# Fetching attention heads one by one with a casting DMA, and running TensorE on ones before the first inputs come

## The chip, the cores and the metric

One core of a Trainium2 chip. The metric is the device time of one execution in microseconds (us). Each kernel was executed several times, with one execution under the hardware profiler; timed kernels were run in rounds beside the kernel before on the same chip. A ratio is the mean time of one kernel's fast runs over the mean of the other's fast runs of the same rounds, so it is not quite the ratio of the medians that are quoted.

## The reference

Attention over 4 batches, 8 heads, 768 positions, 64 columns a head; some heads ("retrieval") see all earlier positions, the others ("streaming") only the first 4 positions and a window of 64. Then a two-layer block on the result:

```python
def reference(q, k, v, is_retrieval, n_sink, window, w_in, w_out):
    scores = q @ k.T / 8                       # per batch and head
    mask = causal where is_retrieval else causal & (sink | window)
    a = softmax(where(mask, scores, -1e9))
    x = (a @ v) as (3072, 512)
    h = x @ w_in                               # 512 -> 2048
    return (h - tanh(h)) @ w_out               # 2048 -> 512, float32
```

q, k, v and the weights come as float32 in device memory.

## The kernel before

The kernel works on 12 tiles of 256 positions (three a batch). A small planner inside it takes every instruction with a guessed duration, simulates the engines, and so fixes each engine's order; at run time each engine goes through its own list in that order. Batch 0 (tiles 0 to 2) takes the heads as they come. From tile 3 on the heads are sorted so that retrieval heads come first ("ranked"), so that half of the head pairs need only the window; the sort is worked out on the chip from the flags, and the rank-to-head table sits in registers.

Before, a ranked tile is fetched by plain DMAs, six a tile, and GpSimd (POOL) then casts float32 to float16 head by head, picking the head by a register:

```python
for i in blocks:                               # 2 blocks of 128 positions, q, k, v each
    op("SP", ..., lambda: nc.sync.dma_start(
        out=raw_of(nm, t)[:, i, h0 : h0 + nh, :],
        in_=src[b, h0 : h0 + nh, s0 : s0 + 128, :].rearrange("h p d -> p h d")))
...
at = bass.ds(regs["POOL"][rank], 1)            # cast_ranked: 8 casts of q and k, 8 of v
nc.gpsimd.tensor_copy(out=t16[t % 2][:, :, :, rank : rank + 1, :],
                      in_=raws["rqk", t][0]()[:, :, :, at, :])
```

Weights and tiles 1 and 2 come by casting DMAs that GpSimd issues. The three forms of them that this document compares:

```python
nc.gpsimd.dma_start(out=t16[...][:, i, x, :, :],              # q, k, v: 128 x 8 runs of 256 B
    in_=src[b, :, s0 : s0 + 128, :].rearrange("h p d -> p h d"))
nc.gpsimd.dma_start(out=w()[:],                               # w_in: 128 x 4 runs of 2 KB
    in_=moe_w_in[:, c0 : c0 + n].rearrange("(cb p) f -> p cb f", p=128))
nc.gpsimd.dma_start(out=w()[:].rearrange("p i m -> p (i m)"), # w_out: 128 runs of 8 KB
    in_=moe_w_out[j * 512 : (j + 1) * 512, :].rearrange("(p i) m -> p (i m)", p=128))
```

After the casts, two DMA transposes a tile (queue SP) put q and k in place, GpSimd "spreads" parts of v into `vf`, and TensorE scores, sums values and runs the two layers.

The softmax here doesn't subtract the row's maximum and nothing guards it: scores larger than these inputs give would overflow.

Of the kernel before, what the change touches and what calls it, by code (L numbers as in the profile page):

```python
# [12 lines left out]
TT = 256  # L13
# [3 lines left out]
class Plan:  # L17
# [16 lines left out]
    def op(self, eng, ns, fn, r=(), w=(), dma=None, prio=None, port=False, after=None, behind=None):  # L34
        i = len(self.ops)
        deps = set() if after is None else {after}
        for k in r:
            if k in self.writer:
                deps.add(self.writer[k])
            if k[0] in self.PSUM:  # L40
                deps.update(j for j in self.readers.get(k, ()) if self.ops[j][0] != eng)
            self.readers.setdefault(k, []).append(i)
# [16 lines left out]
    def run(self):  # L59
# [45 lines left out]
        while len(order) < n:  # L105
# [34 lines left out]
            for u in followers[i]:  # L140
                ready[u] = max(ready[u], t + ns)
                left[u] -= 1
                if not left[u]:
                    enqueue(u)
            if dma:
                packets, each = dma
                rings["POOL" if e == "POOL" else "SP"].append(
                    [i, t + ns + (1200 if e == "POOL" else 300), each, packets * each / 16]
                )
            else:  # L150
                finish(i, t + ns + self.RESULT[e])
# [6 lines left out]
def kernel(  # L158
# [35 lines left out]
    RAW, PT, XB, GB, XTB, THB, OB = 2, 3, 3, 3, 3, 3, 3  # L194
# [28 lines left out]
    gate = const.tile([1, 1], FP16, name="gate")  # L223
# [33 lines left out]
    def program(first):  # L257
# [30 lines left out]
        def paired(nm, t):  # L288

            return nm != "v" and t == 0  # L290

        def load(t, names="qkv", halves=(None,), blocks=range(NB), after=None):

            b, g = divmod(t, NG)
            for half in halves:
                h0, nh = (0, H) if half is None else (half * HH, HH)
                for nm in names:
                    src = {"q": q, "k": k, "v": v}[nm]
                    tag = "rv" if nm == "v" else "rqk"
                    if (tag, t) not in raws:  # L300
                        idx = rot[tag] = rot.get(tag, -1) + 1
                        shape = [128, NB, H, D] if nm == "v" else [128, NB, 2, H, D]
                        raws[tag, t] = (
                            lazy(raw_pool, shape, FP32, tag, f"raw_{tag}{t}"), idx
                        )
                    if paired(nm, t):
                        op(
                            "SP", max(420, 128 * nh * 1.1),
                            lambda nm=nm, src=src, h0=h0, nh=nh: nc.sync.dma_start(
                                out=raw_pairs(nm, t)[:, h0 : h0 + nh, :, :].rearrange(  # L310
                                    "p h e d -> p h (e d)"
                                ),
                                in_=src[b, h0 : h0 + nh, g * TT : (g + 1) * TT, :].rearrange(
                                    "h (p e) d -> p h (e d)", e=NB
                                ),
                            ),
                            w=[
                                key for x in (range(2) if half is None else (half,))
                                for key in raw_keys(nm, t, x)
                            ],  # L320
                            dma=(128 * nh, 26.0), after=after,
                        )
                        continue
                    for i in blocks:
                        s0 = g * TT + i * 128
                        op(
                            "SP", max(420, 128 * nh * 1.1),
                            lambda nm=nm, i=i, src=src, s0=s0, h0=h0, nh=nh: nc.sync.dma_start(
                                out=raw_of(nm, t)[:, i, h0 : h0 + nh, :],
                                in_=src[b, h0 : h0 + nh, s0 : s0 + 128, :].rearrange("h p d -> p h d"),  # L330
                            ),
                            w=[
                                key for x in (range(2) if half is None else (half,))
                                for key in raw_keys(nm, t, x, (i,))
                            ],
                            dma=(128 * nh, 18.3), after=after,
                        )
# [13 lines left out]
        def raw_keys(nm, t, half, blocks=range(NB)):  # L351
            tag = "rv" if nm == "v" else "rqk"
            return [(tag, raws[tag, t][1], nm, half, i) for i in blocks]
# [11 lines left out]
        def load_cast(t, w_after=(), names="qkv"):  # L365

            b, g = divmod(t, NG)
            for nm in names:
# [13 lines left out]
                if nm == "v":  # L382
                    for i in range(NB):
# [3 lines left out]
                            dma=(128 * H, 18.5),  # L387
                        )
                    continue
                for i in range(NB):  # L390
                    behind(
                        930, lambda fn=fn, i=i: fn((i,)), r=w_after,
                        w=[key for half in range(2) for key in t16_keys(nm, t, half, (i,))],
                        dma=(128 * H, 18.5),
# [37 lines left out]
        for half in range(2):  # L432
            load(0, "qk", (half,))
            load(0, "v", (half,))
        if first:

            op("POOL", 204, lambda: nc.gpsimd.memset(ones[:], 1.0), w=["ones"])
            op(
# [98 lines left out]
        def by_rank(after):  # L537

            def dve(ns, fn, r, w):
                op("DVE", ns, fn, r=r, w=w, after=after)  # L540
# [82 lines left out]
                r=["A4", "A40", "A41", "A43"], w=["mS"], port=True, after=after,  # L623
# [4 lines left out]
                r=["mS3"], w=["mS"], port=True, after=after,  # L628
            )
            for e, et in (("POOL", Engine.Pool), ("DVE", Engine.DVE)):  # L630
# [7 lines left out]
                op(e, 900, get, r=["perm"], w=["regs" + e])  # L638
# [9 lines left out]
        def t16_keys(nm, t, half, blocks=range(NB)):  # L648
            return [("t16", t % 2, nm, half, i) for i in blocks]

        def cast_qk(t, engines, halves=range(2)):

            for half in halves:
                for nm, es in zip("qk", engines):
                    hs = slice(half * HH, half * HH + HH)
                    cast_op(
                        es[half], NB * HH * D,
                        lambda nm=nm, hs=hs: t16[t % 2][:, :, "qk".index(nm), hs, :],
                        lambda nm=nm, hs=hs: raw_of(nm, t)[:, :, hs, :],
                        r=raw_keys(nm, t, half), w=t16_keys(nm, t, half),  # L660
                    )

        def cast_ranked(t):
# [4 lines left out]
            for half in range(2):  # L668
                for nm in ("qk", "v"):
                    for rank in range(half * HH, half * HH + HH):  # L670

                        def fn(nm=nm, rank=rank):
                            at = bass.ds(regs["POOL"][rank], 1)
                            if nm == "v":
                                nc.gpsimd.tensor_copy(  # L675
                                    out=v1s[b]()[:, lo : lo + NB, rank : rank + 1, 0:D],
                                    in_=raw_of("v", t)[:, :, at, :],
                                )
                            else:
                                nc.gpsimd.tensor_copy(  # L680
                                    out=t16[t % 2][:, :, :, rank : rank + 1, :],
                                    in_=raws["rqk", t][0]()[:, :, :, at, :],
                                )

                        op(
                            "POOL", 300 if nm == "v" else 430, fn,
                            r=["regsPOOL"] + [
                                key for x in range(2) for n_ in nm for key in raw_keys(n_, t, x)
                            ],
                            w=[("v1", b, g, half)] if nm == "v" else [  # L690
                                key for n_ in nm for key in t16_keys(n_, t, half)
                            ],
                            port=True,
                        )
            for i in range(NB):

                def turn(i=i):
# [7 lines left out]
                    r=[key for half in range(2) for n_ in "qk" for key in t16_keys(n_, t, half)],  # L705
# [83 lines left out]
        def cast_v(t, engines=("POOL", "POOL"), halves=range(2)):  # L789
# [5 lines left out]
            for half in halves:  # L795
# [4 lines left out]
                    r=raw_keys("v", t, half), w=[("v1", b, g, half)],  # L800
# [27 lines left out]
        def st_T(n, eq="DVE", ek="DVE"):  # L828
            t, hp = divmod(n, HP)
            b, g = divmod(t, NG)  # L830
            for x, (nm, e) in enumerate((("q", eq), ("k", ek))):
# [9 lines left out]
                def turn(x=x, tp=tp):  # L841
# [7 lines left out]
                    "PE", 112, turn, r=t16_keys(nm, t, hp * 2 // HP) + ["ident"], w=[key],  # L849
# [412 lines left out]
        cast_qk(0, (("ACT", "ACT"), ("ACT", "DVE")), (0,))  # L1262
        load_cast(1, [("rv", 0, "v", 0, 1)], "qk")
# [10 lines left out]
        cast_v(0, ("POOL", "POOL"), (0,))  # L1274
        cast_qk(0, (("ACT", "ACT"), ("ACT", "DVE")), (1,))
# [8 lines left out]
        cast_v(0, ("POOL", "POOL"), (1,))  # L1284
# [16 lines left out]
        else:  # L1301
            load(2)
            scale_v(0, "POOL")
        scale_v(1)
        if first:

            def wait_tile_2():
                nc.sync.dma_start(out=gate[:], in_=t16[0][0:1, 0, 1, 0, 0:1])

# [133 lines left out]
```

## Time and profile before

| | kernel before |
|---|---|
| time, median of 3 | 238.7 us |
| span of the profiled execution | 236.7 us |
| TensorE busy | 221.5 us |
| first real matmul / first hidden-layer matmul | 6.0 / 18.9 us |
| GpSimd busy | 90.5 us |

The prediction shows the page, the table of stretches and TensorE's waits. In a line of groups the columns are: line, engine, operation, output and input, count, then busy us, mean ns of one, then the idle time of the engine just before them and what ended it. The casts that the change removes, and the casting DMAs' time on GpSimd:

```profile
L680 POOL CAST t<-raw_rqk 128x256 f16 x72 | 28.5, 440 | 63.3 <-DMA raw_rqk<-in_k_dram 48.1 <-PE sc L941 15.2
L675 POOL CAST v<-raw_rv 128x128 f16 x72 | 21.1, 335 | 4.2 <-DMA raw_rv<-in_v_dram 4.2
...
L378 POOL DMA_DIRECT2D t<-in_q_dram x4 | 3.8, 963 | 0.0
...
L401 POOL DMA_DIRECT2D win<-in_moe_w_in_dram x4 | 3.0, 762 | 0.0
L415 POOL DMA_DIRECT2D wout<-in_moe_w_out_dram x4 | 2.3, 573 | 1.8 <-DMA wout<-in_moe_w_out_dram 1.6 <-DMA t<-in_q_dram 0.3
```

A run is one contiguous piece of device memory: a DMA of 1024 runs (here q) holds GpSimd for 0.96 us.

### The profile page before, as it was taken

How to read it: one execution, taken by the hardware profiler on the slowest of the kernel's cores; microseconds unless marked ns; L12 is line 12 of the kernel's file. 1: busy time of each engine (PE TensorE's matmuls, PEld its weight loads, DVE VectorE, ACT ScalarE, POOL GpSimd, SP SyncE). 2: the span in 40 equal slices, each digit the busy share in tenths (PEclk: the TensorE clock that was granted, in tenths of full speed). 3: DMA queues.
4: the chain of work that ended last, by engine and by line, in shares of the span. 5: the costliest groups of instructions: out<-in, count | busy, mean ns of one | idle time of the engine just before them, and what ended most of it. 6: DMA issues, size and time to landing. Idle time of an engine off the chain costs nothing. (4 is left out here: it accounts for less than half of the span.)

```text
span 236.7 us, 5895 instructions
## 1 busy us (share of the span) xinstructions
PE 221.5 (94%) x2220; PEld 157.8 (67%) x2220; DVE 139.0 (59%) x343; ACT 143.6 (61%) x221; POOL 90.5 (38%) x218
## 2 busy tenths in 40 slices
PE   0889899999999999999999999999999999999991
PEld 0346687756776777777676777776776777777661
DVE  1856665864488657767666655667766546443300
ACT  3668677884588387466686649537759464444320
POOL 5999420089818068480814904606300000000000
PEclk9999999999999999999999999999999999999999
DMA  5999999999997999979989695998712101310121
GB/s 128 209 140 172 204 181 204 197 228 224 206 225 182 151 248 184 227 153 206 239 168 214 136 186 130 186 171 179 134 47 66 38 31 47 90 38 9 44 89 51
DMA packets 108130, 35.29 MB, mean 149 GB/s; under 512 B 100290, under 2 KB 104642, under 8 KB 108098
## 3 DMA queue, kind: packets, MB, share of 16 engines
q1 hardware_dynamic: 92642, 28.98, 60.5%
q0 software_dynamic: 15168, 5.77, 20.7%
q8 instruction: 18, 0.29, 0.5%
q10 hardware_dynamic: 288, 0.14, 0.2%
q14 instruction: 14, 0.11, 0.2%
HBM read 27.27 MB, written 6.29 MB: 142 GB/s over the span
## 5 line engine op out<-in xcount | busy, mean ns | idle before, releaser
L1135 PE MATMUL ph<-xT,win 128*128 128x256 f16 x768 | 101.7, 273 | 0.6 <-DMA win<-in_moe_w_in_dram 0.3
L1194 PE MATMUL po<-wout,gt 128*128 128x512 f16 (+1 forms) x400 | 98.0, 371 | 0.3 <-ACT ot L1170 0.3
L1148 ACT ACTIVATE th<-ph 128x512 f32<-128x512 f32 x96 | 57.6, 601 | 59.6 <-PE ph L1135 58.2
L1155 DVE SCALAR_TENSOR_TENSOR gt<-th,ph 128x512 f16<-128x512 f32 x96 | 65.4, 684 | 44.9 <-ACT th L1148 44.4
L1135 PEld LDWEIGHTS <-win 128*128 128x128 f16 x768 | 80.0, 114 | 13.0 <-issue 1.9
L961 ACT ACTIVATE pt<-sc 128x1024 f16<-128x1024 f32 (+1 forms) x78 | 68.5, 926 | 11.4 <-PE sc L941 10.9
L1194 PEld LDWEIGHTS <-gt 128*128 128x128 f16 x400 | 36.4, 98 | 24.6 <-issue 0.9
L680 POOL CAST t<-raw_rqk 128x256 f16 x72 | 28.5, 440 | 63.3 <-DMA raw_rqk<-in_k_dram 48.1
L1030 PEld LDWEIGHTS <-pt 128*128 128x128 f16 x552 | 25.9, 98 | 10.4 <-issue 0.9
L1030 PE MATMUL av<-v,pt 128*128 128x65 f16 x304 | 26.0, 195 | 0.1
L941 PE MATMUL sc<-qk 64*128 64x128 f16 (+1 forms) x412 | 23.8, 240 | 1.7 <-DVE qk L826 1.7
L941 PEld LDWEIGHTS <-qk 64*128 64x128 f16 x412 | 13.7, 94 | 13.5 <-issue 8.9
L675 POOL CAST v<-raw_rv 128x128 f16 x72 | 21.1, 335 | 4.2 <-DMA raw_rv<-in_v_dram 4.2
L1060 DVE TENSOR_TENSOR x16t<-av,rinv 128x128 f32 x72 | 20.8, 289 | 2.3 <-DVE rinv L1050 0.3
L1030 PE MATMUL av<-vf,pt 128*128 128x65 f16 x248 | 19.6, 193 | 0.0
L1170 ACT ACTIVATE ot<-po 128x512 f32<-128x512 f32 (+1 forms) x24 | 14.3, 596 | 8.5 <-PE po L1194 8.4
L996 DVE TENSOR_TENSOR pt<-pt,m 128x1024 f16<-128x1024 f16 x16 | 12.3, 768 | 8.0 <-ACT pt L961 8.0
L1050 DVE RECIPROCAL rinv<-av 128x4 f32<-128x4 f32 x48 | 8.6, 179 | 13.4 <-PE av L1030 13.4
L986 DVE TENSOR_TENSOR pt<-pt,mS 128x512 f16<-128x512 f16 x24 | 9.8, 449 | 6.7 <-ACT pt L961 6.7
L843 PEld LDWEIGHTS <-t 128*128 128x128 f16 x48 | 3.9, 107 | 8.9 <-ACT t L644 6.8
L523 DVE TENSOR_SCALAR m<-A,thr 128x512 f16<-128x512 f16 x16 | 7.4, 501 | 1.7 <-PE sc L928 1.2
L751 POOL TENSOR_TENSOR vf<-v,rflagr 128x260 f16<-128x260 f16 x12 | 7.5, 634 | 0.0
(95 smaller groups left out, 90.8 us busy)
## 6 DMA issues: line engine op xcount, KB each, us to landing
out_dram<-ot SPq DMA_DIRECT2D x23, 256.0 KB, 2.3
raw_rqk<-in_q_dram SPq DMA_DIRECT2D x20, 256.0 KB, 4.7
raw_rqk<-in_k_dram SPq DMA_DIRECT2D x20, 256.0 KB, 4.5
raw_rv<-in_v_dram SPq DMA_DIRECT2D x18, 256.0 KB, 4.4
win<-in_moe_w_in_dram POOLq DMA_DIRECT2D x4, 512.0 KB, 8.8
wout<-in_moe_w_out_dram POOLq DMA_DIRECT2D x4, 512.0 KB, 12.4
raw_rv<-in_v_dram SPq DMA_DIRECT2D x4, 128.0 KB, 4.7
t<-in_q_dram POOLq DMA_DIRECT2D x4, 128.0 KB, 9.5
```

Of the source, the lines that this page charges most:

```text
L675: nc.gpsimd.tensor_copy(out=v1s[b]()[:, lo : lo + NB, rank : rank + 1, 0:D], in_=raw_of("v", t)[:, :, at, :],)
L680: nc.gpsimd.tensor_copy(out=t16[t % 2][:, :, :, rank : rank + 1, :], in_=raws["rqk", t][0]()[:, :, :, at, :],)
L941: nc.tensor.matmul(out=sc()[:, hh, o : o + nb * 128].rearrange("p (i c) -> p i c", c=128), lhsT=ks.rearrange("p i c -> p (i c)")[p_, jb * ...
L961: lambda pt=pt, gi=gi, wid=wid, sc=sc: nc.scalar.activation(out=pt()[:, :, 512 * gi : 512 * gi + wid], in_=sc()[:, :, 0:wid], func=AF.Exp, ...
L996: nc.vector.tensor_mul(out=pv, in0=pv, in1=m4[:, h0 : h0 + 2, 256:512].unsqueeze(2).to_broadcast([128, 2, 2, 256]),)
L1030: nc.tensor.matmul(out=av()[:, i, hh, :], lhsT=pt()[:, hh, co : co + 128], rhs=vv, start=(jb == first_jb), stop=(jb == qb),)
L1060: nc.vector.tensor_mul(out=x16s[t]()[:, :, at, :], in0=av()[:, :, hh : hh + 1, 0:D], in1=rinv()[:, :, hh : hh + 1].unsqueeze(3).to_broadca ...
L1135: nc.tensor.matmul(out=ph()[:, j, :], lhsT=w()[:, cb, c0 + fb % 4 : c0 + 512 : 4], rhs=xTs[t]()[:, cb, :], start=(cb == 0), stop=(cb == HP ...
L1148: lambda: nc.scalar.activation(out=th()[:], in_=ph()[:], func=AF.Tanh, scale=1.0 / XS),
L1155: lambda: nc.vector.scalar_tensor_tensor(out=gts[t]()[:, u * FU : (u + 1) * FU, :], in0=th()[:], scalar=-XS, in1=ph()[:], op0=ALU.mult, op ...
L1170: nc.scalar.activation(out=ot()[:, c0:c1], in_=po()[:, c0:c1], func=AF.Copy, scale=1.0 / XS)
L1194: nc.tensor.matmul(out=po()[:, c0:c1], lhsT=gts[t]()[:, f, ts * 128 : ts * 128 + 128], rhs=w_out_t[f // 4]()[:, f % 4, c0:c1], start=(f == ...
```

## The change

Its intent: take the casts of batches 1 to 3 off GpSimd by letting the DMA cast in flight, head by head, into the place of the rank; start the first tile two heads at a time; let TensorE multiply a tile of ones until q and k come, so that its clock is up by then. Six small parts go with it. Its core (cuts marked):

```diff
@@ planner: nothing slips in between two chained DMA issues
-                ready[u] = max(ready[u], t + ns)
+                ready[u] = max(ready[u], free[e])
@@ buffers
-    RAW, PT, XB, GB, XTB, THB, OB = 2, 3, 3, 3, 3, 3, 3
+    RAW, PT, XB, GB, XTB, THB, OB = 1, 4, 3, 3, 3, 3, 3
@@ first tile by pairs of heads
-        for half in range(2):
-            load(0, "qk", (half,))
-            load(0, "v", (half,))
+        for names, pairs in [("qk", (0,)), ("qk", (1,)), ("v", (0, 1)), ("qk", (2, 3)), ("v", (2, 3))]:
+            load(0, names, pairs)
@@ run-up
+            wm, key = bank([128, 512], FP32, "o", "warm")
+            def run_up():
+                for _ in range(10):
+                    nc.tensor.matmul(out=wm()[...], lhsT=ones[:], rhs=ones[:]...to_broadcast([128, 4, 128]),
+                                     start=True, stop=True)
+            op("PE", 4000, run_up, r=["ones"], w=[key])
@@ ranked tiles: cast_ranked goes, load_ranked comes
+                for rank in range(H):
+                    def fn(nm=nm, src=src, rank=rank):
+                        at = bass.ds(regs["POOL"][rank], 1)
+                        ...
+                        nc.gpsimd.dma_start(
+                            out=o,          # v1 or t16, in the place of the rank
+                            in_=src[b, at, g * TT : (g + 1) * TT, :].rearrange(
+                                "h (i p) d -> p i (h d)", p=128))
+                    behind(380, fn, r=["regsPOOL"], ..., dma=(NB * 128, 14.0), after=PACE.get((t, nm)))
@@ pacing: q, k of tile t+2 behind the scores of tile t's third head pair, v behind its fourth
+                        names = ["", "", "qk", "v"][hp]
+                            PACE[t + 2, nm] = first_S[t * HP + hp] if t > 1 else None
+                        if ranked(t + 2):
+                            load_ranked(t + 2, names)
@@ the sort of heads one tile earlier
-                if first and fast and (t, hp) == (2, 0):
+                if first and fast and (t, hp) == (1, 0):
... (keys by head pair instead of half, casts of tile 0 dealt to ACT and DVE by pair, a gate on
     tile 1's load until the second pair of k is in, guessed DMA costs)
```

## The prediction

> **What bounds the kernel now.** I read the summary page first, for who is full and when.
>
> ```profile
> PE 221.5 (94%) x2220; PEld 157.8 (67%) x2220; DVE 139.0 (59%) x343; ACT 143.6 (61%) x221; POOL 90.5 (38%) x218
> PE   0889899999999999999999999999999999999991
> ```
>
> The kernel runs on TensorE's time: empty slice 0, ragged slices 1 to 3, full from then to the last slice. A busy TensorE is not one at its peak, so I went next to the table of stretches, with bounds chosen at the first transpose (6), the first hidden-layer matmul (19) and the end of the loads.
>
> ```profile
> 0.00:6.00 6.00, 0.00 (x0) 0.00 (x0) 1.03 (x7) 2.10 (x3) 3.09 (x16) 1.00 0.53 130
> 6.00:19.00 13.00, 11.12 (x97) 5.66 (x98) 9.44 (x27) 8.94 (x16) 12.77 (x17) 1.00 1.58 167
> 19.00:30.00 11.00, 9.78 (x124) 7.26 (x125) 7.09 (x19) 8.34 (x14) 7.53 (x9) 1.00 1.28 197
> 30.00:40.00 10.00, 9.70 (x101) 8.13 (x99) 5.86 (x12) 7.09 (x14) 1.23 (x3) 1.00 1.67 192
> 40.00:70.00 30.00, 29.33 (x330) 20.78 (x329) 19.07 (x60) 21.21 (x33) 15.98 (x43) 1.00 1.12 216
> 70.00:160.00 90.00, 89.73 (x939) 64.84 (x936) 59.73 (x142) 57.31 (x86) 44.08 (x117) 1.00 0.97 185
> 160.00:232.00 72.00, 71.81 (x646) 51.12 (x638) 36.40 (x81) 38.57 (x60) 5.86 (x17) 1.00 0.25 68
> ```
>
> Columns: stretch and length, then busy us and instructions of PE, PEld, DVE, ACT, POOL, then clock, DMA share, GB/s. To see how much of "busy" is work, I took the matmuls of each stretch from the groups by form and charged each its array time[...]. Sums: 5.9 us of work in the 13 of 6 to 19; 9.0 in the 11 of 19 to 30; 9.7 in 10; 29.0 in 30; then 91 in 90 and 72.5 in 72, that is, full. So what can be won is 6 us of empty start, 7 us in the head, 2 in 19 to 30, about 1.3 up to 70, and the 5 us after the last matmul, which the change doesn't touch. Nothing can be won from 70 to 232.
>
> Then the waits of TensorE over the span:
>
> ```profile
> PE tp0q L843 <- ACT t L644: 6.0, 1, 6.0
> PE sc L941 <- DVE qk L826: 1.7, 3, 0.7
> PE xp L1108 <- DVE x L1074: 1.1, 3, 0.6
> PE tp0k L843 <- ACT t L644: 0.5, 1, 0.5
> PE ph L1135 <- DMA win<-in_moe_w_in_dram: 0.3, 1, 0.3
> ```
>
> The casts and loads of batches 1 to 3 stand nowhere in it: POOL itself waits 48.1 us for the raw q and k, and its casts still come early enough.
>
> [...]the same 128x128 transpose takes 300 ns at 7 us and 219 ns from 15 us on, and the clock's record begins near 15 us. [...]
>
> **The change, part by part.**
>
> Run-up. Ten 512-column matmuls of ones: ones are ready at 1.1 us; 10 x 427 ns at half clock[...] is 4.3 us, so about 1.3 to 5.6 us, which ends about when the first cast is done. It costs at most some 0.3 us. The clock should then be full by about 5 to 8 us instead of 15. What half clock cost between 6 and 15: 3584 mask columns, 1536 column-slots of scores, 2304 of transposes and 780 of values[...]: 1.5 + 0.6 + 1.0 + 0.3 = 3.4 us of TensorE. The path through the head (transpose, copy, mask and score, Exp, value, reciprocal, scale, transpose, copy) waits on other engines in between, DVE 9.44 and ACT 8.94 of 13 us, so I count half: **1.7 us**.
>
> Pair by pair start. Now q's four heads land at 5.33 us, k's at 6.27 (0.94 later, of which 0.51 is the later issue), both cast on ACT one after the other (617 ns each), so k's first transpose starts at 6.95. Two heads are half the bytes (about 0.4 us less in flight), the cast is about 0.38 us instead of 0.62, and k's goes to DVE beside q's on ACT: first k transpose about 5.9, **1.0 us** earlier. Not all of it is sure: the masks of the first pair are built on DVE from 5.82, and the second half of q and k still lands near 8.3 to 9.5 us.
>
> POOL's order. The schedule lets nothing slip in between two chained DMA issues any more. Now it does, when POOL is full (12.77 of 13):
>
> ```profile
> 11.13 0.76 POOL L401 DMA_DIRECT2D win<-in_moe_w_in_dram  x1
> 11.90 1.06 POOL L810 TENSOR_TENSOR vf<-v,rflag 128x520 f16<-128x520 f16 x1
> 12.90 0.95 POOL L378 DMA_DIRECT2D v<-in_v_dram  x1
> 13.88 1.06 POOL L810 TENSOR_TENSOR vf<-v,rflag 128x520 f16<-128x520 f16 x1
> ```
>
> The two scalings put off v and the next w_in by 2.1 us, and the bytes moved fall to 6 to 76 GB/s between about 12.8 and 13.8 us, against 150 to 200 around it. Without that the second w_in, which TensorE waited for at 23.7, comes 1 to 2 us earlier, as it must if the earlier head is to be kept. Of the 2 us lost in 19 to 30 I count **0.7 us**.
>
> Loads with cast by head. It removes 72 casts of q and k (28.5 us) and 72 of v (21.1 us) from POOL, all of it beside a full TensorE, and adds 9 tiles x 3 x 8 = 216 DMAs of 256 runs. From 0.96 us for 1024 and 0.57 for 512 runs, one of 256 is about 0.4 us (an estimate): 86 us, so POOL goes from 90 to about 127 us busy. Its tightest stretch is a tile's 24 issues (9.6 us) and 2 to 3 us of spreads against 10 to 26 us per tile with loads asked for two tiles ahead. It fits. Each run is 256 B either way, and the casting queue took 3298 runs in 3 us at its best, 0.9 ns each, where the plain one took 2984 in 4 us, so the DMA engines get no fuller. On the path: **0**.
>
> The rank computation moved one tile earlier, the deeper pt buffers and single raw buffer: 17 small DVE instructions of 0.15 to 0.23 us in another place, **0**.
>
> Sum: 1.7 + 1.0 + 0.7 = 3.4 us, from 238.7 to **235.3 us**, 1.4% less.
>
> **The rivals.** (a) The head is held by data: w_in comes at 11.13 + 5.9 = 17.0 us by its landing time, tile 1 behind it; an earlier chain then meets its DMA wait. For it: DMA is asked for more than it has from 9 us on, and POOL is full. Against it: only 0.3 us of wait for w_in today, and attention of tile 1 can fill in. It would leave 1 to 1.5 us: 237.4. (b) TensorE was the true limit of the head, so all 3.4 us of half clock come off and the earlier start with it: about 5 us, 233.5. For it: 11.12 of 13 busy. Against: DVE's 9.4 us in the head stay, and they are strung one after another. (c) POOL becomes the bound: a head's address comes from a register, and if one such issue took over 0.8 us, 216 of them would pass 170 us with spreads on top, tiles would come late, and TensorE would wait in 50 to 190: 240 and more. For it: no such DMA is in this trace. Against: the issue times above and the planner's own 380 ns. (d) All of it is hidden and the time stays at 238: against it, the head is the one stretch in which TensorE is not full, so what is saved there moves everything after.
>
> **Range and chances.** Main case 3.4 us with some 1.3 us either way from how much of the half clock lies on the path; (a) pulls up, (b) down; (c) has a few per cent. Range 232.8 to 237.9. 2% faster is below 233.9, which needs most of (b): 0.22. Slower by 2% needs (c): 0.03. Within: 0.75.
>
> **What would show it.** First real transposes at about 5.5 us, and 219 ns rather than 300 within 2 us of them; first hidden-layer matmul at 15.5 to 17 instead of 18.93; no vf scaling between w_in and v on POOL; TensorE's last matmul 3 to 4 us earlier, the stretches from 70 us on as full as before; POOL near 127 us and 0.4 us an issue; no wait of TensorE on qk or v above 1 us after 45 us. The prediction is wrong if the first hidden-layer matmul stays near 18 with waits on DMA, if TensorE's clock is still half at 10 us, or if TensorE waits for ranked tiles.

(The sum came to 1.7 + 1.0 + 0.7 = 3.4 us, so 238.7 to 235.3. What the two traces show: at full clock, matmuls that follow one another start 56 ns apart with 128 columns, 109 with 256, 162 with 384 and 216 with 512, value matmuls 30 ns apart; score matmuls start in twos, 2 to 4 ns apart, 56 ns from one two of 128 columns to the next. Charged with these, the work of the six stretches from 6 us on is 5.6, 8.3, 9.1, 26.9, 85.8 and 69.9 us (an estimate from the trace before), a little less than the recorded sums, which charged more for value matmuls: the head is more than half empty and the last two stretches nearly full either way. At half clock it is 320 ns with 384 columns and 427 with 512, 0.41 us more per thousand columns, so the 3.4 us of half clock in the run-up part hold. That ten matmuls bring the clock up by 5 to 8 us was the estimate; in the changed kernel it reads full from 5.1 us. So were the 0.4 us in flight and the 0.38 us of a cast; the changed kernel shows 3.1 us from issue to landing instead of 4.8, and 0.41 us a cast on ScalarE.)

## The result

295.38 us median (294.29 to 295.79, 4 runs) against 238.63: ratio 1.236 (95% interval 1.231 to 1.241), 24% slower. Executions over 1.5% slower than the fastest of the same kernel are left out of the means. The prediction was 235.3 with a range of 232.8 to 237.9, and 0.03 on slower.

The page of the changed kernel, the lines that answer to those of before:

```profile
PE 236.6 (81%) x2230; PEld 163.3 (56%) x2230; DVE 140.6 (48%) x344; ACT 143.2 (49%) x222; POOL 197.7 (68%) x291
## 2 busy tenths in 40 slices
PE   7779999795094399795099999299379999999993
...
POOL 6993859699999699799699399699799500000000
PEclk9859999999579589999569999989859999999999
```

TensorE's row now has holes in its middle, where it was full; GpSimd's row is nearly full up to the slice where the holes end; and in several holes TensorE's granted clock falls too. The table of stretches (columns as in the prediction) puts sizes on it:

```profile
0.00:6.00 6.00, 4.73 (x17) 2.00 (x18) 2.65 (x12) 2.66 (x6) 3.50 (x18) 1.00 0.54 136
6.00:19.00 13.00, 9.11 (x87) 4.49 (x84) 10.18 (x30) 7.02 (x15) 12.89 (x16) 0.73 1.60 185
19.00:30.00 11.00, 10.01 (x105) 6.65 (x104) 7.12 (x28) 7.90 (x13) 5.23 (x8) 0.85 1.45 196
...
40.00:70.00 30.00, 28.03 (x328) 20.12 (x326) 19.04 (x49) 20.48 (x31) 25.43 (x37) 1.00 0.82 76
70.00:160.00 90.00, 59.52 (x564) 40.68 (x565) 35.74 (x83) 36.24 (x53) 82.39 (x119) 0.81 0.87 91
160.00:232.00 72.00, 59.65 (x549) 41.27 (x547) 34.30 (x85) 34.67 (x52) 60.51 (x87) 0.91 0.91 97
```

Up to 70 us the two kernels are within 2 us of each other. From 70 to 160 TensorE does 564 matmuls instead of 939, while GpSimd goes from 44 to 82 of 90 us. The time is lost exactly in the stretches in which the prediction said that nothing could be won; that something could be lost there it put down as rival (c), with a chance of 0.03. TensorE's longest waits, and GpSimd's own:

```profile
PE sc L951 <- DMA qk<-t: 23.5, 6, 10.5
PE ph L1145 <- DMA xT<-x16t: 21.7, 3, 9.9
```

```profile
POOL vf L780 <- DMA v<-in_v_dram: 15.3, 5, 4.8
POOL vf L769 <- DMA v<-in_v_dram: 4.3, 3, 2.1
POOL vf L760 <- DMA v<-in_v_dram: 4.0, 5, 1.7
```

(Columns: waiter, what it waited for, us in total, times, longest us.) TensorE waits for the transposed q and k of a ranked tile, or for the attention output of one: both mean that the tile came late. GpSimd waits for nothing long except its own v. Together TensorE is idle 56.1 us instead of 15.2 and busy 236.6 us instead of 221.5 (4.2 us of it are the ones; most of the rest is the same work at half clock after the holes: from 70 us on, 22.9 us of TensorE's busy time lie where the clock's record reads half). Those two differences, 40.9 and 15.1, are the 56.0 us by which the span grew.

The groups say what fills GpSimd:

```profile
L685 POOL DMA_DIRECT2D t<-in_q_dram x72 | 52.2, 752 | 5.0 <-DMA wout<-in_moe_w_out_dram 2.6
L685 POOL DMA_DIRECT2D v<-in_v_dram x72 | 52.4, 831 | 0.0
L685 POOL DMA_DIRECT2D t<-in_k_dram x72 | 52.0, 781 | 0.0
```

216 issues of 0.75 to 0.83 us (0.72 from one to the next): 157 us, where the casts that they replace took 50. One tile in GpSimd's timeline (start, duration, engine, line, what, count, idle before):

```profile
101.40 5.74 POOL L685 DMA_DIRECT2D t<-in_q_dram  x8 [0.29 <-issue]
107.08 5.79 POOL L685 DMA_DIRECT2D t<-in_k_dram  x8
112.77 5.85 POOL L685 DMA_DIRECT2D v<-in_v_dram  x8
118.99 1.65 POOL L760 TENSOR_TENSOR vf<-v,rflagr 128x260 f16<-128x260 f16 x2 [0.38 <-DMA v<-in_v_dram]
121.63 1.04 POOL L769 COPY vf<-v 64x1040 f16<-64x1040 f16 x1 [0.98 <-DMA v<-in_v_dram]
122.73 0.95 POOL L722 COPY qk<-qk 128x256 f16<-128x256 f16 x2
123.75 0.61 POOL L780 COPY vf<-v 64x260 f16<-64x260 f16 x1
124.39 5.79 POOL L685 DMA_DIRECT2D t<-in_q_dram  x8
```

The tile's 24 issues run from 101.4 to 118.6 us, 17.2 us; its spreads and waits take 5.8 more, and the next tile's q starts 23.0 us after this one's. From 101.40 to the last tile's start at 213.26 that is five tiles in 111.9 us, 22.4 us a tile. TensorE's own pace in the kernel before is 12 tiles between 18.9 and 231.9 us, 17.7 us a tile. So from 33 us, where the first of these issues stands, GpSimd sets the pace; its last one ends at 230.5 us, and what TensorE still has to do then takes it to 288. A better order in GpSimd's list could not have saved it: from 33.4 to 230.5 us GpSimd is busy for 172.7 of 197.1 us, which without any wait is still 19.2 us for each of the nine ranked tiles (an estimate from this trace).

The head (up to the first hidden-layer matmul) did not gain either: the first real transposes come at 5.33 us at full clock, as predicted, but the first hidden-layer matmul comes at 20.7 us, later than the 18.9 of before. The clock shows one reason; the first w_in is none, as it had landed at 17.8 us. The same pair of mask matmuls, in TensorE's timeline:

```profile
10.58 0.49 PE L938 MATMUL sc<-m,ident 128*128 128x384 f16 x2
...
12.59 1.01 PE L938 MATMUL sc<-m,ident 128*128 128x512 f16 x2 [0.29 <-ACT pt L971]
```

The second has a third more columns and takes twice as long; the clock's record in the trace reads full from 5.1 us, half from 12.0, full again from 22.2 us.

### The profile page after: what moved, and what is told of

It is laid out like the page before. It is cut to its first block, busy times and chain, and to the rows that moved or that the text cites. A ratio compares the mean times of both kernels' runs of the same rounds, so it can differ in the third digit from the quotient of the medians.

```text
span 292.7 us, 6262 instructions
## 1 busy us (share of the span) xinstructions
PE 236.6 (81%) x2230; PEld 163.3 (56%) x2230; DVE 140.6 (48%) x344; ACT 143.2 (49%) x222; POOL 197.7 (68%) x291
## 5 line engine op out<-in xcount | busy, mean ns | idle before, releaser
L1145 PE MATMUL ph<-xT,win 128*128 128x256 f16 x768 | 107.4, 283 | 21.7 <-DMA xT<-x16t 21.7
L1145 PEld LDWEIGHTS <-win 128*128 128x128 f16 x768 | 82.2, 116 | 39.2 <-DMA xT<-x16t 22.0
L1204 PE MATMUL po<-wout,gt 128*128 128x512 f16 (+1 forms) x400 | 102.2, 381 | 0.0
L685 POOL DMA_DIRECT2D t<-in_q_dram x72 | 52.2, 752 | 5.0 <-DMA wout<-in_moe_w_out_dram 2.6
L685 POOL DMA_DIRECT2D v<-in_v_dram x72 | 52.4, 831 | 0.0
L685 POOL DMA_DIRECT2D t<-in_k_dram x72 | 52.0, 781 | 0.0
L951 PE MATMUL sc<-qk 64*128 64x128 f16 (+1 forms) x412 | 25.6, 253 | 25.6 <-DMA qk<-t 23.5
L951 PEld LDWEIGHTS <-qk 64*128 64x128 f16 x412 | 15.2, 99 | 39.3 <-DMA qk<-t 16.7
L1040 PE MATMUL av<-v,pt 128*128 128x65 f16 x304 | 26.7, 199 | 0.0
L1040 PE MATMUL av<-vf,pt 128*128 128x65 f16 x248 | 19.9, 195 | 0.0
L1180 ACT ACTIVATE ot<-po 128x512 f32<-128x512 f32 (+1 forms) x24 | 14.3, 595 | 8.1 <-PE po L1204 8.1
L780 POOL COPY vf<-v 64x260 f16<-64x260 f16 (+1 forms) x9 | 4.7, 518 | 15.5 <-DMA v<-in_v_dram 15.3
```

The costliest lines, as they stand in the source:

```text
L685: nc.gpsimd.dma_start(out=o, in_=src[b, at, g * TT : (g + 1) * TT, :].rearrange("h (i p) d -> p i (h d)", p=128),)
L951: nc.tensor.matmul(out=sc()[:, hh, o : o + nb * 128].rearrange("p (i c) -> p i c", c=128), lhsT=ks.rearrange("p i c -> p (i c)")[p_, jb * ...
L1040: nc.tensor.matmul(out=av()[:, i, hh, :], lhsT=pt()[:, hh, co : co + 128], rhs=vv, start=(jb == first_jb), stop=(jb == qb),)
L1145: nc.tensor.matmul(out=ph()[:, j, :], lhsT=w()[:, cb, c0 + fb % 4 : c0 + 512 : 4], rhs=xTs[t]()[:, cb, :], start=(cb == 0), stop=(cb == HP ...
L1180: nc.scalar.activation(out=ot()[:, c0:c1], in_=po()[:, c0:c1], func=AF.Copy, scale=1.0 / XS)
L1204: nc.tensor.matmul(out=po()[:, c0:c1], lhsT=gts[t]()[:, f, ts * 128 : ts * 128 + 128], rhs=w_out_t[f // 4]()[:, f % 4, c0:c1], start=(f == ...
```

## The experiments

Theory 1: GpSimd's time per DMA issue. A by-head casting DMA holds GpSimd about 0.72 us, 24 of them a tile are too many, and TensorE starves. Theory 2: not the number of issues, but loads asked for too late, or data that the casting queue brings too slowly. Theory 3: the head and TensorE's clock. Inside theory 1, two sub-theories: 1a, the cost is fixed per DMA; 1b, it comes from the address in a register.

### Everything but the by-head fetch: head_only

```diff
-                            load_ranked(t + 2, names)
+                            for nm, i in PIECES[hp]:      # as in the kernel before
+                                load(t + 2, nm, blocks=(i,), after=gated if t == 1 else first_S[...])
+                        fs.append(lambda t=t: cast_ranked(t + 1))   # before turn_ranked
-    RAW, PT, ... = 1, 4, ...
+    RAW, PT, ... = 2, 3, ...
```

(Shortened; the cast of the kernel before and its gate on tile 3's first loads come back too.)

> The changed kernel with batches 1 to 3 fetched as before (plain DMA, then head-by-head casts on GpSimd); run-up, pairwise start and order of issues stay. Theory 1 (GpSimd's rate of issuing by-head DMAs starves TensorE): 234 to 241 us, waits of TensorE on qk and xT under 3 us in total, and no half clock after 25 us. Theory 3[...]: 255 us or more. My own prediction for the head alone was 235.3; the head as seen in the changed kernel (first hidden-layer matmul at 20.7 instead of 18.9) says rather 239.

Measured: 237.27 us median of 4 (236.50 to 238.72) against 238.8, ratio 0.994 (0.988 to 1.001). A repeat on the same chip, of five rounds:

> head_only once more, on the same chip as the two above and in more rounds: 236.5 to 238.5 us as before.

Measured: 237.96 us, ratio 0.9964 (0.9935 to 0.9993). TensorE from 70 to 160 us is full again:

```profile
70.00:160.00 90.00, 89.88 (x937) 64.54 (x937) 58.94 (x139) 57.36 (x85) 47.00 (x125) 1.00 1.02 193
```

So the whole loss of 57 us comes with the by-head fetch (the buffer counts also go back in this edit, but halves12 below keeps the changed ones and is fast), and theory 3 falls. The rest of the change is worth 0.4 to 0.6%, some 1 us, instead of the 3.4 I had summed for it.

### The same bytes in fewer issues: whole6 and halves12

Both keep the changed kernel's pacing, bytes and runs, and issue 6 or 12 casting DMAs a tile instead of 24. Both give a wrong result, since the heads come in natural order and fall under the wrong masks. The work did not get cheaper by that: ScalarE's 78 Exp take 925 ns each in the changed kernel, 930 in whole6 and 928 in halves12. The planner was told other durations with them (760 ns an issue for halves12, 1860 for a pair of issues in whole6, 380 in the changed kernel), and so dealt another order.

```diff
-                for rank in range(H):             # 24 a tile: 256 runs each
+                for i in range(NB):               # whole6: 8 heads x 128 rows, 1024 runs each
+                for i, h0 in [...]:               # halves12: 4 heads x 128 rows, 512 runs each
```

> The changed kernel with the same pacing, but each tile of batches 1 to 3 fetched with cast in 6 DMAs of 8 heads and 128 rows (1024 runs of 256 B each, 0.9 us each in the trace) in natural order instead of 24 by-head ones: the result is wrong on purpose (heads under the wrong masks), the bytes, runs and work are the same. Theory 1: GpSimd spends 5.4 us a tile instead of 17.3, time 234 to 242. Theory 2 (loads asked for too late, or the casting queue's data too slow, whatever the number of issues): 270 us or more.

> The changed kernel with 12 casting DMAs a tile of 4 heads and 128 rows (512 runs each), natural order, so wrong on purpose. Theory 1 (mostly a fixed cost per DMA on GpSimd): 0.75 to 0.85 us an issue, half the changed kernel's GpSimd time per tile (9.6 instead of 17.4 us), time 244 to 258 us, between whole6 (246.8) and the changed kernel (295.4) and much nearer to the first. If a DMA's cost went with its runs: 1.5 us an issue or no gain.

Measured: whole6 246.83 us median of 4 (fast runs 244.80, 245.22 and 248.44, ratio of these 1.036; one slow run of 248.59), halves12 239.29 us in its one run. Both miss the intervals given, whole6 above it and halves12 below. GpSimd's groups, first of whole6, then of halves12:

```profile
L686 POOL DMA_DIRECT2D t<-in_q_dram x18 | 16.3, 908 | 0.2
L686 POOL DMA_DIRECT2D v<-in_v_dram x18 | 16.1, 916 | 0.0
L686 POOL DMA_DIRECT2D t<-in_k_dram x18 | 15.9, 898 | 0.0
L757 POOL TENSOR_TENSOR vf<-v,rflagr 128x260 f16<-128x260 f16 x12 | 7.5, 629 | 29.8 <-DMA v<-in_v_dram 29.8
```

```profile
L685 POOL DMA_DIRECT2D t<-in_q_dram x36 | 27.4, 777 | 0.8 <-issue 0.3 <-PE ph L1141 0.3
L685 POOL DMA_DIRECT2D v<-in_v_dram x36 | 27.2, 804 | 0.2
...
L756 POOL TENSOR_TENSOR vf<-v,rflagr 128x260 f16<-128x260 f16 x12 | 7.5, 648 | 7.3 <-DMA v<-in_v_dram 7.3
```

And the stretch of halves12 in which the changed kernel loses most:

```profile
70.00:160.00 90.00, 88.99 (x916) 64.06 (x914) 55.26 (x131) 57.21 (x85) 67.80 (x97) 1.00 1.38 138
```

Twice the runs in one DMA cost the same 0.78 us, and four times 0.91. Halving the number of issues takes off 56 us: theory 2 falls and theory 1 stands, since pacing, bytes, runs and queue are the same. (The planner's guess is truer in halves12, 760 ns against the 777 to 804 shown, than in the changed kernel, 380 against 752 to 831; a changed kernel planned with 720 ns was not run. By the 19.2 us a tile above it would still be bound by GpSimd.) I had expected whole6, with the fewest issues, to be the faster of the two; its fast runs are 5.5 to 9.2 us above halves12. Its GpSimd is not short of time: it waits 29.8 us (halves12: 7.3) in front of the spreads for v, which lands 7.4 us after its issue there (4.4 in halves12, 3.8 in the changed kernel), and its loads of the next tile stand behind those spreads in the same list. So small pieces had a worth of their own on landing in these runs. How much of the difference is that, and how much the planner's other order, these runs don't separate.

### The address: static24

```diff
-                        at = bass.ds(regs["POOL"][rank], 1)
+                        at = slice(PERM[rank], PERM[rank] + 1)    # PERM = [0, 2, 6, 1, 3, 4, 5, 7]
```

> The changed kernel with the 24 by-head DMAs at constant addresses (the ranks of the given flags) instead of a register's. Theory 1a (a DMA has a large fixed cost on GpSimd whatever its address): 0.6 to 0.75 us an issue, time 265 to 296 us. Theory 1b (the register's address is what costs): 0.4 us an issue, as I had estimated, and 235 to 245 us.

Measured: 294.31 us in one run, correct.

```profile
L685 POOL DMA_DIRECT2D v<-in_v_dram x72 | 52.5, 832 | 0.0
L685 POOL DMA_DIRECT2D t<-in_q_dram x72 | 52.2, 752 | 4.2 <-DMA wout<-in_moe_w_out_dram 2.7 <-PE tp L854 1.0 <-issue 0.2
```

The same issues to within a nanosecond in the mean (752 and 832 ns against 752 and 831). The register costs nothing here; 1b falls, 1a stands.

### Only v by head: cast_dma_v

head_only, with v of the ranked tiles by 8 casting DMAs a tile and q and k as in the kernel before.

> The changed kernel with only v of batches 1 to 3 fetched by head with cast (8 DMAs a tile), q and k as before. Theory 1 (GpSimd's time per tile against TensorE's 18.6 us): 8 x 0.73 + 8 x 0.40 casts + 3 us of spreads = 12 us a tile fits, so 236 to 243 us. If by-head DMAs hurt in another way than by their number (order, landing, pacing), over 250 us.

(TensorE's time for a tile is 17.7 us by the reckoning above, not 18.6.)

Measured: 244.12 us in one run. 8 issues a tile fit, as theory 1 has it, but the result is 1 us above the interval given; TensorE waits 3.2 us for attention outputs, and GpSimd now waits for three sorts of DMA in one list. By number of issues a tile the series is 0: 237.3 to 238.0, 6: 246.8, 8 (with casts): 244.1, 12: 239.3, 24: 295.4. It isn't a line: up to 12 issues something else, the order perhaps, makes a few us. Between 12 and 24 nothing was run.

### What the run-up is worth: four kernels

> As head_only, without the ten matmuls of ones. If the run-up is worth something net, this is 1 to 2 us slower than head_only; if the clock it buys is lost again at 12.6 us, as the changed kernel's trace shows, the two are within 0.7 us, and in this one the clock is released near 15 us as in the kernel before.

Measured: 239.40 us (239.19 to 239.71), ratio 1.002 (0.997 to 1.007); head_only 237.27. That looked like 2.1 us for the run-up. The counterpart, the kernel before with the run-up added:

> The kernel before with the ten matmuls of ones alone. head_only against head_no_runup gave 2.1 us for the run-up; if that is its own worth, this is 236 to 237.5 us (1.2 to 2.5 below the kernel before), with first transposes at 220 ns. If the pairwise start is what lets the early clock be used, it is within 0.8 us of the kernel before.

Measured: 241.96 us, ratio 1.015 (1.012 to 1.017), slower by 3.5 us. Both readings were of something else. The run-up was an operation in the planner's list, and with it there or not there the planner deals a different order to every engine: in before_runup the first w_in is issued at 13.7 us instead of 11.1 (one casting DMA has moved to 3.9 us, to the front of GpSimd's list, and behind it the list waits 2.5 us for the raw v). So both were done again with the planner left unaware:

```diff
@@ before_runup_same_order: in the function that emits the first transpose, unknown to the planner
+                    if first and n == 0 and x == 0:
+                        wm = ps.tile([128, 512], FP32, tag="o", ...)
+                        for _ in range(10): nc.tensor.matmul(out=wm[...], lhsT=ones[:], rhs=ones[:]..., ...)
@@ head_no_runup_same_order: the operation stays in the list, and emits nothing
-                for _ in range(10):
+                for _ in range(0):
```

> The kernel before with the ten matmuls of ones, but put in ahead of the first transpose without the planner's knowledge, so that every engine keeps the order of the kernel before (in before_runup the planner dealt the whole schedule anew: the first w_in was issued at 13.7 us instead of 11.1). If the run-up itself helps, 235.5 to 238 us, that is 0.5 to 3 below the kernel before, and the 241.96 of before_runup came from its other order. If the run-up hurts or is nothing, 238.2 to 239.5.

> head_only with its ten matmuls of ones left out, the order of everything else kept. Against head_only_again it gives the run-up's worth in the new head: 1 to 2.5 us slower if it helps; within 0.5 us if the 2.1 us between head_only and head_no_runup were the planner's other order.

Measured: before_runup_same_order 238.86 us, ratio 1.0016 (0.998 to 1.005); head_no_runup_same_order 237.50 us, ratio 0.9952 (0.993 to 0.998), against 0.9964 for head_only_again in the same rounds. Either way round, the run-up is worth nothing that five rounds can see; the intervals leave room for at most some 0.7 us (an estimate from them), not for 1.7. The stretches of before_runup_same_order show a reason:

```profile
6.00:13.00 7.00, 5.88 (x41) 2.82 (x42) 5.22 (x13) 5.04 (x9) 6.83 (x10) 0.60 1.75 190
13.00:19.00 6.00, 5.18 (x61) 3.00 (x60) 4.04 (x15) 4.08 (x9) 5.98 (x8) 0.90 1.35 140
```

The clock was full from 4.0 us on, as intended, but only to 7.4; then it was half until 14.3 us, and without the run-up it had come at 14.95. (The 1.00 that the kernel before shows in these stretches is a gap in its record, which begins at 14.95 us; its 300 ns transposes show the half clock.)

### Relief for VectorE, and a TensorE kept busy: head_calm and head_calm_warm

```diff
@@ head_calm = head_only with
-                if first and fast and (t, hp) == (1, 0):        # sort of heads back at tile 2
+                if first and fast and (t, hp) == (2, 0):
-                    fs.append(lambda: masks(thr, "thr", range(H)))
+                    fs.append(lambda: masks(thr, "thr", range(H), after=first_S[HP + 1]))
@@ head_calm_warm = head_calm with the mask matmuls of head pairs 1 to 5 done three times over
+                        for x in range(2 * times):              # times = 3 if 0 < n < 6 else 1
+                            hh = x % 2
+                            nc.tensor.matmul(..., start=True, stop=x < 2 * times - 2)
```

On VectorE's mask builds, the traces show 345 ns each at 45 us with GpSimd idle and 508 in the head beside it (kernel before), and 1467 for the two from 13.2 us on in the changed kernel, while GpSimd issues DMAs and scales v. How much of that is GpSimd's doing was not tested by itself.

> head_only with VectorE relieved in the head: the rank computation back at tile 2, and the rebuilding of the masks not before the scores of the sixth head pair. In head_only VectorE's mask pair took 1.79 us at 12.5 us and a rank step 0.96 us beside GpSimd, and TensorE waited 1.04 and 0.96 us for VectorE's copies right behind. If these set the head, the first hidden-layer matmul comes 1 to 2 us before head_only's 18.4 and the time is 235 to 236.5; if w_in's landing or the clock sets it, within 0.7 us of head_only (237.3).

> head_calm with the mask matmuls of head pairs 1 to 5 done three times over (each time from zero, so the result is unchanged), to keep TensorE from idling in the head. If the clock falls back to half at 18.5 us[...], the first hidden-layer matmuls take 1.06 us for eight instead of 1.69, granted clock 1.0 in 19 to 30 us instead of 0.85, and 1 to 1.5 us are won over head_calm; if the clock falls back anyway, it is equal or 0.5 us slower.

(The first case is the one in which the extra matmuls keep the clock up. That sparse work takes it down was the guess; no run here shows it.)

Measured: head_calm 238.06 us (235.25 to 238.65), ratio 0.9957 (0.992 to 1.000), so not told apart from head_only. head_calm_warm 240.78 us, ratio 1.010 (1.007 to 1.013), 2.7 us above head_calm, which neither case expected. In head_calm's profiled run the clock stayed full from 6.2 us to the last matmul, even without the extra matmuls (this is one execution; the mean clocks of the six go from 0.988 to 1.000), and the first hidden-layer matmul still came at 18.8 us. TensorE's timeline shows what it was waiting for:

```profile
16.73 0.59 PE L970 MATMUL sc<-m,ident 128*128 128x512 f16 x2 [0.62 <-ACT pt L1003]
...
18.77 1.06 PE L1177 MATMUL ph<-xT,win 128*128 128x256 f16 x8 [1.45 <-DMA win<-in_moe_w_in_dram]
```

The first w_in, issued at 10.37 us, landed 8.3 us later, at 18.7. In that profile, with a full clock and a calmer VectorE, the head ends on the landing of w_in. In the profiles of all the kernels here it lands at 16.7 to 19.7 us; only in head_calm and head_no_runup_same_order does the first hidden-layer matmul follow within 0.1 us. In the others it comes 0.5 to 3 us later (head_only: 16.7 and 18.6), so there something else ends the head, and these runs don't settle what. head_calm_warm has a full clock as well and is slower: its extra matmuls stand in the chain of the head, and its first hidden-layer matmul comes at 19.9 us; its order is another one too, so no more is read from it.

## Why the prediction was wrong

**The step that failed** is in the part "Loads with cast by head": "From 0.96 us for 1024 and 0.57 for 512 runs, one of 256 is about 0.4 us (an estimate)". The 0.57 us are w_out's, and w_out's DMA has 128 runs of 8 KB, not 512: I had taken the 512 from the packet count that the planner is told, not from the access pattern. (The page counts 15168 packets in the casting queue; 12 x 1024 for q, k and v and 4 x 512 for each weight would be 16384, more than there are.) The form that does have 512 runs, w_in, stood in the same profile at 0.76 us. With the three points rightly laid down (128 runs 0.57, 512 runs 0.76, 1024 runs 0.90 to 0.96) the cost is nearly all fixed, and 256 runs come out between 0.57 and 0.76. Measured: 0.75 to 0.83 us as the profile gives it, 0.72 from one to the next; static24 showed that it is not the register, halves12 that twice the runs cost no more. I then leaned on "the planner's own 380 ns" as a second witness, but that is a guess in the kernel's source, and no measurement.

**The budget was a second fault.** Even 0.72 us would not have set off its alarm: it held the total ("if one such issue took over 0.8 us, 216 of them would pass 170 us") against the span, and set the limit at 0.8. What counts is the tile: 17.2 us of issues, and on average 5.2 us of spreads and of waits for v's landing that stand in the same in-order list, are 22.4 us against TensorE's 17.7. "Its tightest stretch is a tile's 24 issues (9.6 us) and 2 to 3 us of spreads against 10 to 26 us per tile" had the right shape; the 9.6 measured 17.2, the landing of v was left out, and the sum was held against a range with 26 in it, where TensorE's 17.7 was the limit.

**The rival was named.** Rival (c), "POOL becomes the bound: ... tiles would come late, and TensorE would wait in 50 to 190: 240 and more", is what happened, and it got 0.03. The evidence asked of the trace was right too: "POOL near 127 us and 0.4 us an issue" came out as 197.7 and 0.72.

**"Nothing can be won from 70 to 232"** was right, and the changed loads lie just there. That TensorE doesn't wait for casts today says that they have slack; it doesn't say that three times their GpSimd time has room.

**DMA engines.** "the DMA engines get no fuller" failed, without cost in time. Their share from 70 to 160 us fell from 0.97 to 0.87 only because the changed kernel did less there; halves12, with the same runs at nearly the old pace, has 1.38 (the share adds up the times of all packets, so it can pass 1). Over the whole span the pages' shares come to 194 us of the 16 engines' time before, 235 in the changed kernel and 239 in halves12. The prediction had counted runs per us of a queue, not the engines' time for a run.

**Run-up, "1.7 us".** The mechanism up to the first transposes was right: at 5.33 us and at 219 ns rather than 300 in the run with the clock up. What failed is "The clock should then be full by about 5 to 8 us instead of 15", read as for good: it fell back at 12.0 us in the changed kernel, at 7.4 us in before_runup_same_order, and the worth is nil (1.0016 and, the other way round, 0.9952 against 0.9964). What takes it down again was not shown: in the changed kernel the longest of TensorE's gaps between 5.3 and 12.0 us was 0.75 us, and of the 11 profiles with the ones in front nine have a granted clock below 1.00 somewhere between 6 and 30 us, while head_calm and head_calm_warm keep 1.00.

**Pair by pair, "1.0 us", and POOL's order, "0.7 us".** Together with the rest of the head they are worth 0.4 to 0.6%, 1 to 1.5 us, by head_only and its repeat, and nothing of that is the run-up. The scalings left the place between w_in and v, as predicted, and the second w_in was issued at 13.3 us instead of 15.8. Rival (a), "The head is held by data", came nearer than my main case: head_calm, with a full clock, stood 1.45 us before w_in, and (a)'s number was 237.4 where head_only and its repeat say 237.3 to 238.0. But in their profiles w_in had landed about 2 us before its first use, so that the number fits is in part luck; what ends the head there stays open.

**Best version.** head_only (0.994 and 0.996 of the kernel before) and head_no_runup_same_order (0.9952, interval 0.9926 to 0.9979) are a little faster than both kernels: the change without its by-head fetch, with or without the ones. That the gain is above zero is shown by the second's interval and by that of head_only's repeat (0.9935 to 0.9993); head_only's first reaches 1.001.

## What to carry to other kernels

Before moving work from an engine's arithmetic to DMAs that the same engine issues, count issues, not bytes or runs (here 0.78 us for 256 and for 512 runs, 0.91 for 1024), and take the issue's cost from rows whose access patterns you have written out; then hold the sum of everything in that engine's list per period of the loop, landing waits included, against the period of the bound engine, not a total against the span. An engine with slack to its waits is not an engine with room (GpSimd here: TensorE waited for none of its casts, and 22.4 us a tile did not fit into 17.7). And where a planner deals the order, a part put in or taken out changes the order everywhere (here the first w_in went from 11.1 to 13.7 us): to measure the part, keep it out of the planner's sight.
